# The last queries' scores put ahead of their pair's scores, a head on each half of the array's columns, and the second batch's attention begun 1.5 steps later

## The chip, the cores and the metric

The kernel runs on one core of a Trainium2 chip. The metric is the time of one execution on the device in microseconds (us). Of the kernel before there are three timed runs, with a median of 1007.72 us (1007.47 to 1007.87), and one profiled execution.

## The reference

Two stages follow each other: attention with a sliding window of 128 positions, then a two-layer MLP.

```python
B, H, S, D = 8, 8, 576, 64
scores = (1 / sqrt(D)) * q @ k.T                 # per batch and head
scores += slopes[h] * -abs(i - j)                # a slope per head
scores = where((i - j >= 0) & (i - j < 128), scores, -1e9)
attn = exp(scores - max(scores)); attn /= sum(attn) + 1e-9
x = (attn @ v), heads side by side               # 4608 tokens x 512
h = x @ w_in                                     # 512 -> 2048
g = h * tanh(softplus(h))                        # "mish"
out = g @ w_out                                  # 2048 -> 512
```

## The kernel before, in words

**Work and tiles.** The 576 tokens of a batch are cut into 512 and 64 left over. A *chunk* of the MLP is the 512 tokens of one batch; the 64 that are left of all eight batches make up a ninth chunk. Each chunk runs `first` (its products are called `h`, 8 steps), then `mish`, then `second` (products `po`, for two halves of the tokens: 32 calls of six matmuls, which are the *steps* of the schedule). Both layers take each f32 number as two parts (`parts`, tile `gg`; for the weights `convert`, tiles `si` and `so`), three products each. The weights come as 64-bit words and are turned into these parts by ScalarE (ACT), VectorE (DVE) and GpSimd (POOL) at the start, beside the first batch's attention, the first layer of chunk 0, and the first 11 steps or so of its second layer.

**Attention.** Heads go in four pairs `p`. A pair has two *units* (`unit(b, p, half)`): half 0 takes the first 256 queries, half 1 the next 256, and each unit its own two PSUM banks (tag `s`, two buffers, which `first` uses too). `last_unit(b, p)` takes the 64 queries left over, both heads in one go: the weights `z` (tile `qd`) hold the two heads' queries in opposite corners of a 128x128 square with zeros elsewhere, so that a product with the stacked keys of both heads gives head 0 in rows 0 to 63 and head 1 in rows 64 to 127. From batch 1 on its scores lie in the first 96 columns of the two banks of the pair's half 0, which that unit leaves free. A unit's stages: scores (TensorE, PE), a reduction on DVE that adds the bias and finds the maximum (`exps`: tiles `pz`, `mx`), the exponential on ACT, `fold` and `scale` (in batch 1 on POOL; from batch 2 on by DVE, whose instructions write `un` as well, and ACT), `weights` (four transposes on PE into the scores' own bank, `s<-ident,pz`, and a DVE product with the masks back into `pz`), `values` (PE, `o`), `split_x`.

**Order.** Attention of batch c+1 runs beside `second` of chunk c. `attention` gives each stage a time in units, the main loop maps it to steps by `begin` and `units`, and the work is recorded in order of these times. PE and the DMA queue of SyncE (SP) keep this order; a scheduler places DVE, ACT and POOL instructions, except while the weights are converted. From batch 2 on, both halves' scores of a pair stand together: half 0, half 1, last unit. I call this group of scores a *visit*. In batch 1 half 1's scores come a unit later. Tiles of the last units carry an `l`: `pz_1l`, `pt_1l`.

Every operation is recorded through `InOrder`, so in the profile all have line 30; instructions are told apart by their tiles. A group `64*128` or `128*64` is a matmul that uses half of the array's rows or half of its columns.

Of the kernel before, what the change touches and what calls it, by code (L numbers as in the profile page):

```python
# [8 lines left out]
F32 = mybir.dt.float32  # L9
# [7 lines left out]
P = 128  # L17
# [24 lines left out]
def attention_mish_mlp(  # L42
# [35 lines left out]
    ps = ctx.enter_context(tc.tile_pool(name="ps", bufs=1, space=bass.MemoryType.PSUM))  # L78
# [12 lines left out]
    for t in vb:  # L91
# [8 lines left out]
    pe, dve, act, pool, sp = engines = [  # L100
        InOrder(tc, e, e in (nc.tensor, nc.sync))
        for e in (nc.tensor, nc.vector, nc.scalar, nc.gpsimd, nc.sync)
    ]
# [97 lines left out]
    qkv = {}  # L201
# [42 lines left out]

    HEAD = [slice(i * D, (i + 1) * D) for i in range(2)]

    def unit(b, p, half):


# [4 lines left out]
        st = {}  # L254
        blocks = (0, 1) if half == 0 else (2, 3)
        name = f"{b}_{p}_{half}"

        def scores():
            qk = qkv[(b, p)][0]
            if b == 0 and (2 * p + half) % 3 == 2:  # L260
                s_ = [ps.tile([P, 512], F32, tag=f"po{i}", name=f"s{name}{i}") for i in range(2)]
            else:
                t = ps.tile([P, 2, 512], F32, tag="s", name=f"s{name}", bufs=2)
                s_ = [t[:, i, :] for i in range(2)]
                if half == 0:
                    qkv[("s", b, p)] = t
            st["s"] = s_
            for a, j in enumerate(blocks):
                n = 256 if j else P
                for i in range(2):  # L270
                    pe.matmul(
                        s_[i][:, 256 * (a + 1) - n : 256 * (a + 1)], lhsT=qk[HEAD[i], 0, j * P : (j + 1) * P],
                        rhs=qk[HEAD[i], 1, (j + 1) * P - n : (j + 1) * P], start=True, stop=True,
                    )
# [92 lines left out]
        times = (0, 0.02, 0.25, 0.7, 0.95, 1.3, 1.99, 2.02)  # L367
        if b == 0:
            times = (0, 0.02, 0.2, 0.75, 0.8, 1.62, 2.3, 2.35)
        elif b > 1:  # L370

            times = (
                (-1, -0.8, -0.7, -0.3, -0.25, 0.7 if p == 1 else 0.65, 0.97, 0.99) if half
                else (0, 0.02, 0.12, 0.4, 0.45, 1.4 if p == 1 else 1.3, 1.96, 1.96)
            )
# [4 lines left out]
    def last_unit(b, p):  # L380

        st = {}
        name = f"{b}_{p}l"

        def scores():
            qk, z = qkv[(b, p)]

            if b == 0:
                st["t"] = ps.tile([P, 512], F32, tag="w", name=f"pt{name}")
                st["s"] = st["t"][:, 192:384].rearrange("p (a n) -> p a n", a=2)  # L390
            else:
                st["s"] = qkv[("s", b, p)][:, :, :96]
            for i in range(2):
                pe.matmul(
                    st["s"][:, i, :], lhsT=z, rhs=qk[:, 1, 384 + 96 * i : 480 + 96 * i],
                    start=True, stop=True,
                )

        def exps():
            mx = at.tile([P, 1], F32, tag="mxl", name=f"mx{name}")  # L400
            sm = st["sm"] = at.tile([P, 1], F32, tag="sml", name=f"sm{name}")
            pz = st["pz"] = at.tile([P, 192], F32, tag="pzl", name=f"pz{name}")
            dve.tensor_tensor_reduce(
                out=pz.rearrange("p (a n) -> p a n", a=2), in0=st["s"],
                in1=nl[:, p, :].rearrange("p (a n) -> p a n", a=2), scale=-SCALE, scalar=3.0e38,
                op0=ALU.add, op1=ALU.min, accum_out=mx,
            )
            act.activation(pz, pz, AF.Exp, bias=mx, scale=-1.0, accum_out=sm)

        def fold():  # L410
            sm, pz = st["sm"], st["pz"]
            act.activation(sm, sm, AF.Copy, bias=1e-9)
            dve.reciprocal(sm, sm)
            un = at.tile([P, 1], F32, tag="unl", name=f"un{name}")
            dve.tensor_tensor_reduce(
                out=pz[:, :64], in0=pz[:, :64], in1=pz[:, P:], scale=sm, scalar=3.0e38,
                op0=ALU.add, op1=ALU.min, accum_out=un,
            )
            act.activation(pz[:, 64:P], pz[:, 64:P], AF.Copy, scale=sm)

        def weights():
            if b:
                st["t"] = ps.tile([P, 512], F32, tag="w", name=f"pt{name}")
            t = st["t"]
            pe.transpose(t[:, :P], st["pz"][:, :P], ident)
            pf = st["pf"] = at.tile([P, 2, 2, 64], F32, tag="pfl", name=f"pf{name}", bufs=1)
            shape = [P, 2, 2, 64]
            dve.tensor_tensor(
                out=pf, in0=t[:, :P].rearrange("p (u i n) -> p u i n", u=1, i=2).to_broadcast(shape),
                in1=masks[:, :, :64].rearrange("p u (i n) -> p u i n", i=1).to_broadcast(shape),  # L430
                op=ALU.mult,
            )

        def values():
            va, vl = qkv[("v", b, p)]
            o = st["t"][:, P : P + LEFT]
            for n, val in enumerate((va[:, 3, :], vl)):
                for i in range(2):
                    pe.matmul(
                        o[HEAD[i]], lhsT=val[:, HEAD[i]], rhs=st["pf"][:, n, i, :],  # L440
                        start=(n == 0), stop=(n == 1), skip_group_check=True,
                    )
            xo = at.tile([P, LEFT], F32, tag="xo", name=f"xo{name}", bufs=5)
            dve.tensor_copy(xo, o)
            sp.dma_start(out=xs[p, :, b * LEFT : (b + 1) * LEFT], in_=xo)

        times = (0.01, 0.5, 0.9, 1.4, 1.995)
        if b == 0:
            times = (0.66, 0.7, 1.1, 1.64, 2.32)
        elif b > 1:  # L450
            times = (0.002, 0.21, 0.5, 1.78 if p == 1 else 1.7, 1.98)
        return list(zip(times, (scores, exps, fold, weights, values)))

    def attention(b):
# [48 lines left out]
    def mish(c, j):  # L503
        f = 2 * (j % 2)
        act.activation(gt[(c, j // 2)][:, f : f + 2, :], hs.pop((c, j)), AF.Mish)
# [58 lines left out]
    def in_order(work):  # L564
        dve.fixed = act.fixed = True
        work()
        dve.fixed = act.fixed = False
# [9 lines left out]
    def convert_at(times, tags, lag, mixed):  # L577
        steps = []
        for m, t in enumerate(times):
            kind, j, a = conv.pop(0)  # L580
            step = convert(kind, j, a, tags[m % len(tags)], mixed and m % 2 == 1)
            steps += list(zip((t - lag, t, t + lag), step))
        return steps
# [7 lines left out]
    for c in range(B + 1):  # L591
        if c == 0:
            act.fixed = True
            steps = convert_at([0.35 * m for m in range(4)], ("po0", "po1"), 0.36, True)
            steps += convert_at([0.35 * m for m in range(4, 22)], ("w", "o"), 0.36, True)
            for j in range(NJ):
                steps += [(j, lambda j=j: first(c, j)), (j + 1.04, lambda j=j: mish(c, j))]
            steps += [(NJ - 1.6, lambda: (parts(c, 0, 0), parts(c, 0, 1)))]
            for _, work in sorted(steps, key=lambda s: s[0]):
                work()  # L600
            load_w(*last_w)
            dve.fixed = act.fixed = False
        else:
            for j in range(NJ):
                if j == NJ - 1:
                    parts(c, 0, 0)
                    parts(c, 0, 1)
                first(c, j)
                mish(c, j)

        n = 4 * NJ
        steps = []
        for m in range(2 * NJ):
            for t in range(2):
                steps.append((2 * m + t, lambda m=m, t=t: second(c, *divmod(m, NJ), t)))
            if m >= 2:
                steps.append((2 * m - 4.1, lambda m=m: parts(c, *divmod(m, NJ))))
        if c == 0:
            for t, work in convert_at([0.3 + 1.35 * m for m in range(len(conv))], ("w", "o"), 1.3, True):
                steps.append((t, lambda work=work: in_order(work)))  # L620
        if c + 1 < B:
            begin, units = (1.4, 8.0) if c else (10.0, 9.0)
            steps += [(begin + (n - 2.1 - begin) / units * s, f) for s, f in attention(c + 1)]
        elif c + 1 == B:
            steps.append((4.5, last_x))
        for _, work in sorted(steps, key=lambda s: s[0]):
            work()
# [63 lines left out]
```

## Time and profile before

| | |
|---|---|
| timed runs, median | 1007.72 us |
| the profiled execution's own time | 1008.28 us |
| its span, first to last instruction | 1006.5 us |
| PE busy | 975.6 us, 97% |
| ACT, DVE, POOL busy | 425.0, 375.4, 262.5 us |
| mean granted clock of TensorE | 0.995 of full speed |

The span is what the views cut up; the 1.8 us around it belong to the execution as well. A row of the timeline merges instructions of one kind that follow each other: its second column runs from the start of the first to the modelled end of the last, so it overlaps the next row, and the distance between two rows' starts is the better measure of what the first one cost.

### The profile page before, as it was taken

To read this page: it belongs to the slowest core of one execution; us is meant where nothing else is said; L and a number is where in the kernel's file an instruction comes from. 1 tells how busy PE (TensorE), PEld (TensorE's weight loads), DVE (VectorE), ACT (ScalarE), POOL (GpSimd) and SP (SyncE) were. 2 spreads that over 40 slices of the span, in tenths; PEclk is the share of its full clock that TensorE was granted. 3 is DMA by queue.
4 is the path that set the end of the run, shared out by engine and by line. 5 is a ranking of instruction groups with operands and counts; after the bars stand their busy time and mean duration, and the time that the engine had idled before them with its cause. 6 is when DMAs were issued, how large, how long until landed. Compare 5 with 4: busy or idle time off the path is not lost.

```text
span 1006.5 us, 14264 instructions
## 1 busy us (share of the span) xinstructions
PE 975.6 (97%) x5280; PEld 783.6 (78%) x5280; DVE 375.4 (37%) x1287; ACT 425.0 (42%) x1117; POOL 262.5 (26%) x230
## 2 busy tenths in 40 slices
PE   6799899999999999999999999999999999999998
PEld 4478677887888778887888788887888788888886
DVE  5797563036600762047402670067304650100000
ACT  5698663245432552245324452264324642321221
POOL 4468752112210321023111221032112211141033
PEclk9999899999999999999999999999999999999999
DMA  8961122003100231012200211022100200000001
GB/s 267 396 218 43 36 88 71 1 25 98 41 33 1 64 99 35 1 42 81 72 1 26 75 61 35 1 64 83 49 1 25 73 26 20 21 21 22 1 5 38
DMA packets 52133, 59.32 MB, mean 59 GB/s; under 512 B 13024, under 2 KB 32608, under 8 KB 52064
## 3 DMA queue, kind: packets, MB, share of 16 engines
q1 hardware_dynamic: 50880, 57.69, 17.8%
q8 instruction: 42, 0.69, 0.3%
q10 hardware_dynamic: 1184, 0.72, 0.2%
q14 instruction: 27, 0.22, 0.1%
HBM read 47.91 MB, written 10.49 MB: 58 GB/s over the span
## 4 chain that ended last, share of the span: by engine, by line
PE 85%; DVE 5%; ACT 4%; DMA 3%; SPq 1%; issue 1%; POOL 1%; ACTq 0%; POOLq 0%
PE h L30 38%; PE po L30 33%; PE s L30 8%; PE o L30 4%; DVE pz L30 3%; ACT pz L30 3%; DMA wi<-in_moe_w_in_dram 2%; DMA wo<-in_moe_w_out_dram 1%; SPq L30 1%; DVE pz_1l L30 1%; ACT gg L30 1%; DMA nb<-in_relb_dram 1%; POOL pz L30 0%; DVE ob L30 0%; DVE ti L30 0%
## 5 line engine op out<-in xcount | busy, mean ns | idle before, releaser
L30 PE MATMUL po<-so,gg 128*128 128x512 f32 x1728 | 421.7, 397 | 0.0
L30 PE MATMUL h<-x,si 128*128 128x512 f32 x1728 | 394.5, 389 | 1.1 <-POOL si L30 1.0
L30 PEld LDWEIGHTS h<-x,si 128*128 128x128 f32 x1728 | 323.9, 188 | 70.1 <-POOL si L30 2.3
L30 PEld LDWEIGHTS po<-so,gg 128*128 128x128 f32 x1728 | 318.9, 189 | 64.6 <-issue 0.7
L30 POOL TENSOR_TENSOR gg<-g,gg 128x512 fp32r<-128x512 f32 x144 | 185.0, 1285 | 675.5 <-ACT gg L30 675.3
L30 DVE CUSTOM_DVE_ANT_0 pz<-s,nb 128x256 f32<-128x256 f32 (+1 forms) x256 | 84.8, 386 | 330.4 <-PE s L30 330.3
L30 ACT ACTIVATE g<-h 128x1024 f32<-128x1024 f32 x72 | 74.1, 1029 | 255.5 <-PE h L30 255.5
L30 ACT ACTIVATE pz<-pz,mx 128x256 f32<-128x256 f32 (+1 forms) x256 | 120.0, 470 | 71.2 <-DVE mx L30 71.2
L30 ACT ACTIVATE gg<-g 128x512 fp32r<-128x512 f32 x144 | 89.8, 625 | 89.2 <-PE po L30 86.1
L30 DVE TENSOR_TENSOR pz<-s,masks 128x1024 f32<-128x1024 f32 x64 | 76.3, 1216 | 7.5 <-PE s L30 5.8
L30 DVE CUSTOM_DVE_ANT_0 pz<-pz,sm 128x128 f32<-128x128 f32 x144 | 62.6, 483 | 1.7
L30 DVE COPY ob<-po 128x512 f32<-128x512 f32 x18 | 12.3, 686 | 128.0 <-PE po L30 128.0
L30 PE MATMUL s<-ident,pz 128*128 128x128 f32 x256 | 43.6, 286 | 10.5 <-POOL pz L30 8.3
L30 ACT ACTIVATE x<-o 128x512 fp32r<-128x512 f32 x32 | 19.0, 594 | 81.0 <-PE o L30 81.0
L30 PE MATMUL o<-pz,va 128*64 128x128 f32 (+1 forms) x560 | 50.9, 322 | 1.4 <-DVE pz L30 1.4
L30 PEld LDWEIGHTS o<-pz,va 128*64 128x64 f32 x560 | 33.6, 136 | 22.7 <-issue 7.3
L30 PE MATMUL s<-qk 64*128 64x128 f32 (+1 forms) x448 | 51.2, 365 | 0.0
L30 PEld LDWEIGHTS s<-ident,pz 128*128 128x128 f32 x256 | 32.1, 143 | 23.4 <-POOL pz L30 10.5
L30 ACT ACTIVATION_READ_ACCUMULATOR pz<-pz,mx 128x1 f32 x256 | 47.9, 187 | 0.0
L30 PEld LDWEIGHTS s<-qk 64*128 64x128 f32 x448 | 36.0, 186 | 7.1 <-issue 3.3
L30 ACT ACTIVATE ob<-po 128x512 f32<-128x512 f32 x18 | 10.7, 597 | 61.0 <-PE po L30 61.0
L30 DVE TENSOR_TENSOR x<-o,x 128x512 fp32r<-128x512 f32 x32 | 22.1, 692 | 12.2 <-ACT x L30 12.2
(134 smaller groups left out, 505.4 us busy)
## 6 DMA issues: line engine op xcount, KB each, us to landing
wi<-in_moe_w_in_dram SPq DMA_DIRECT2D x16, 512.0 KB, 10.8
wo<-in_moe_w_out_dram SPq DMA_DIRECT2D x16, 512.0 KB, 10.2
out_dram<-ob SPq DMA_DIRECT2D x32, 256.0 KB, 2.0
qk<-in_q_dram SPq DMA_DIRECT2D x28, 288.0 KB, 3.0
qk<-in_k_dram SPq DMA_DIRECT2D x28, 288.0 KB, 3.3
va<-in_v_dram SPq DMA_DIRECT2D x28, 256.0 KB, 2.9
first<-in_q_dram SPq DMA_DIRECT2D x4, 288.0 KB, 4.0
first<-in_k_dram SPq DMA_DIRECT2D x4, 288.0 KB, 4.2
```

The source lines that it names most:

```text
L30: ins = method(*args, **kwargs)
```

## The change

Three things change. In `last_unit`, from batch 1 on, the scores are computed by four matmuls with 64 of the weights' columns each (one per head and per bank) in place of two with 128. Their time in the schedule goes from just behind the pair's scores to just ahead of them, and so `last_unit` takes the banks and half 0 picks them up. And batch 1's attention begins at step 11.5 of chunk 0's second layer instead of step 10; its end stays, so a unit gets 18.4/9 steps where it had 19.9/9. Batch 0 keeps its order and its two matmuls.

```diff
+    def score_banks(name):
+        return ps.tile([P, 2, 512], F32, tag="s", name=f"s{name}", bufs=2)
...
-                t = ps.tile([P, 2, 512], F32, tag="s", name=f"s{name}", bufs=2)
+                t = qkv.pop(("s", b, p), None) or score_banks(name)
                 s_ = [t[:, i, :] for i in range(2)]
-                if half == 0:
-                    qkv[("s", b, p)] = t
...
+                parts = [slice(0, P)]
             else:
-                st["s"] = qkv[("s", b, p)][:, :, :96]
-            for i in range(2):
-                pe.matmul(
-                    st["s"][:, i, :], lhsT=z, rhs=qk[:, 1, 384 + 96 * i : 480 + 96 * i],
-                    start=True, stop=True,
-                )
+                t = qkv[("s", b, p)] = score_banks(f"{b}_{p}_0")
+                st["s"] = t[:, :, :96]
+                parts = HEAD
+            for a in range(2):
+                for r in parts:
+                    pe.matmul(
+                        st["s"][r, a, :], lhsT=z[:, r], rhs=qk[:, 1, 384 + 96 * a : 480 + 96 * a],
+                        start=True, stop=True, skip_group_check=True,
+                    )
...
-        times = (0.01, 0.5, 0.9, 1.4, 1.995)
+        times = (-0.001, 0.5, 0.9, 1.4, 1.995)
...
-            times = (0.002, 0.21, 0.5, 1.78 if p == 1 else 1.7, 1.98)
+            times = (-0.01, 0.21, 0.5, 1.78 if p == 1 else 1.7, 1.98)
...
-            begin, units = (1.4, 8.0) if c else (10.0, 9.0)
+            begin, units = (1.4, 8.0) if c else (11.5, 9.0)
```

On PE, at the start of batch 1's attention in chunk 0 (`so_951` to `so_953` are the last three pieces of the second layer's weights, `s_0_0` and `s_0_1` the banks of pair 0's two halves, `pt_0l` the last unit's transpose), the kernel before has:

```order
L30 MATMUL s_0_0_1094<-qk_0_390 128x128 x2
L30 MATMUL s_0_0_1094<-qk_0_390 128x256 x2
L30 MATMUL s_0_0_1094<-qk_0_390,qd_83 128x96 x2
L30 MATMUL po_0_1_972<-so_951,gg_0_5_1037 128x512 x6
L30 MATMUL po_0_0_959<-so_952,gg_0_6_1058 128x512 x6
L30 MATMUL s_0_1_1143<-qk_0_390 128x256 x4
L30 MATMUL s_0_0_1094<-ident,pz_0_0_1103 128x128 x4
L30 MATMUL po_0_1_972<-so_952,gg_0_6_1058 128x512 x6
```

The changed kernel has at the same place on PE, from the same point of the second layer on:

```order
L30 MATMUL po_0_1_972<-so_951,gg_0_5_1037 128x512 x6
L30 MATMUL s_0_0_1102<-qk_0_390,qd_83 64x96 x4
L30 MATMUL s_0_0_1102<-qk_0_390 128x128 x2
L30 MATMUL s_0_0_1102<-qk_0_390 128x256 x2
L30 MATMUL po_0_0_959<-so_952,gg_0_6_1058 128x512 x6
L30 MATMUL po_0_1_972<-so_952,gg_0_6_1058 128x512 x6
L30 MATMUL s_0_1_1151<-qk_0_390 128x256 x4
L30 MATMUL po_0_0_959<-so_953,gg_0_7_1085 128x512 x6
L30 MATMUL s_0_0_1102<-ident,pz_0_0_1113 128x128 x4
```

Two steps of `po` have moved ahead of the first transposes, the second of them with `so_953`; between the scores of `s_0_0` and these transposes three steps stand where two stood.

On PE in a visit of batch 2 (pair 1; `qd_84` marks the last unit's scores), before:

```order
L30 MATMUL pt_0l<-pf_0l,vb_87 64x64 x2
L30 MATMUL s_1_0_2028<-qk_1_1543 128x128 x2
L30 MATMUL s_1_0_2028<-qk_1_1543 128x256 x2
L30 MATMUL s_1_1_2033<-qk_1_1543 128x256 x4
L30 MATMUL s_1_0_2028<-qk_1_1543,qd_84 128x96 x2
L30 MATMUL po_0_1_1866<-so_950,gg_0_4_1941 128x512 x6
```

And the same visit on PE now:

```order
L30 MATMUL pt_0l<-pf_0l,vb_87 64x64 x2
L30 MATMUL s_1_0_2035<-qk_1_1551,qd_84 64x96 x4
L30 MATMUL s_1_0_2035<-qk_1_1551 128x128 x2
L30 MATMUL s_1_0_2035<-qk_1_1551 128x256 x2
L30 MATMUL s_1_1_2047<-qk_1_1551 128x256 x4
```

The last unit's scores went from the end of the visit to its start, as four matmuls; from batch 2 on nothing else moved on PE.

On DVE, the reductions behind that visit, before (a row in brackets waits for a semaphore):

```order
L30 ISA pz_1_0_2042,mx_1_0_2040<-s_1_0_2028,nb 128x256
L30 ISA mx_1_0_2040 128x1
L30 ISA pz_1_1_2059,mx_1_1_2057<-s_1_1_2033,nb 128x256 [waits DVE_49]
L30 ISA mx_1_1_2057 128x1
L30 ISA pz_1_1_2059,mx_1_1_2057<-s_1_1_2033,nb 128x256
L30 ISA mx_1_1_2057 128x1
L30 ISA pz_1l,mx_1l<-s_1_0_2028,nl 128x192
L30 ISA mx_1l 128x1
```

And the reductions on DVE behind that visit now:

```order
L30 ISA pz_1_0_2054,mx_1_0_2052<-s_1_0_2035,nb 128x128 [waits DVE_49,PE_49]
L30 ISA mx_1_0_2052 128x1
...
L30 ISA pz_1l,mx_1l<-s_1_0_2035,nl 128x192
L30 ISA mx_1l 128x1
L30 ISA pz_1_1_2071,mx_1_1_2069<-s_1_1_2047,nb 128x256 [waits DVE_49,PE_49]
L30 ISA mx_1_1_2069 128x1
```

The last unit's reduction stands before half 1's, and half 1's has a wait of its own for PE, which it did not have: before, the wait of half 0's first reduction covered the whole visit.

## Rows read from the trace of the kernel before

**Rows 1.** The page: busy time of each engine; the chain that ended last, by engine.

```profile
PE 975.6 (97%) x5280; PEld 783.6 (78%) x5280; DVE 375.4 (37%) x1287; ACT 425.0 (42%) x1117; POOL 262.5 (26%) x230
...
PE 85%; DVE 5%; ACT 4%; DMA 3%; SPq 1%; issue 1%; POOL 1%; ACTq 0%; POOLq 0%
```

**Rows 2.** Timeline of PE, rows with idle time: start, us, engine, operation, [idle <-releaser].

```profile
116.87 1.11 PE L30 MATMUL s<-ident,pz 128*128 128x128 f32 x4 [4.30 <-POOL pz L30]
...
150.07 0.65 PE L30 MATMUL s<-ident,pz 128*128 128x128 f32 x4 [0.56 <-POOL pz L30]
```

**Rows 3.** Waits of PE from 200 us to the end: us in total, times, longest.

```profile
PE s L30 <- DVE un L30: 2.2, 6, 0.4
PE o L30 <- DVE pz L30: 1.4, 6, 0.2
```

**Rows 4.** Stretches: us, busy time of PE, PEld, DVE, ACT, POOL, PEclk, DMA, GB/s.

```profile
112.50:115.50 3.00, 0.07 (x2) 0.00 (x0) 0.87 (x5) 2.77 (x10) 2.89 (x3) 1.00 0.58 183
115.50:122.30 6.80, 5.43 (x16) 4.36 (x17) 3.48 (x11) 2.86 (x10) 5.86 (x6) 0.50 0.04 11
```

**Rows 5.** Timeline of PE behind that idle time, and the same work in batch 2.

```profile
117.63 2.91 PE L30 MATMUL po<-so,gg 128*128 128x512 f32 x6
...
120.41 2.52 PE L30 MATMUL po<-so,gg 128*128 128x512 f32 x6
...
253.96 0.60 PE L30 MATMUL s<-ident,pz 128*128 128x128 f32 x4
254.31 1.64 PE L30 MATMUL po<-so,gg 128*128 128x512 f32 x6
...
256.25 1.63 PE L30 MATMUL po<-so,gg 128*128 128x512 f32 x6
```

**Rows 6.** Timeline of ACT, then of POOL, at the start of batch 1's attention.

```profile
109.37 1.28 ACT L30 ACT_TABLE_LOAD   x1
110.67 0.40 ACT L30 ACTIVATE pz<-pz,mx 128x128 f32<-128x128 f32 x1
...
112.96 0.64 ACT L30 ACTIVATE so<-wo 128x512 fp32r<-128x512 f32 x1
...
112.61 0.73 POOL L30 TENSOR_TENSOR pz<-pz 128x256 f32<-128x256 f32 x1 [2.15 <-ACT pz L30]
...
114.52 1.29 POOL L30 TENSOR_TENSOR so<-wo,so 128x512 fp32r<-128x512 f32 x1
115.77 1.04 POOL L30 TENSOR_TENSOR pz<-pz,sm 128x512 f32<-128x512 f32 x1
```

**Rows 7.** Timeline of DVE and POOL in pair 1 of batch 3.

```profile
348.74 1.43 DVE L30 CUSTOM_DVE_ANT_0 pz<-pz,sm 128x128 f32<-128x128 f32 x1
...
348.72 1.29 POOL L30 TENSOR_TENSOR gg<-g,gg 128x512 fp32r<-128x512 f32 x1 [0.48 <-ACT gg L30]
```

**Rows 8.** Timeline of PE: a visit of batch 3 (pair 2), and rows of batch 1.

```profile
354.67 0.29 PE L30 MATMUL pt_1l<-pf_1l,vb 128*64 128x64 f32 x4
354.89 1.79 PE L30 MATMUL s<-qk 64*128 64x128 f32 x16
356.61 0.69 PE L30 MATMUL s<-qk,qd 128*128 128x96 f32 x4
357.07 7.10 PE L30 MATMUL po<-so,gg 128*128 128x512 f32 x30
...
123.56 0.28 PE L30 MATMUL pt_0l<-pf_0l,va 128*64 128x64 f32 x4
123.67 0.29 PE L30 MATMUL pt_0l<-pf_0l,vb 128*64 128x64 f32 x4
123.89 0.93 PE L30 MATMUL s<-qk 64*128 64x128 f32 x8
...
125.21 1.63 PE L30 MATMUL po<-so,gg 128*128 128x512 f32 x6
...
130.75 1.67 PE L30 MATMUL po<-so,gg 128*128 128x512 f32 x6
```

**Rows 9.** Timeline of DVE: the first reduction behind the visit of rows 8.

```profile
357.33 0.29 DVE L30 CUSTOM_DVE_ANT_0 pz<-s,nb 128x128 f32<-128x128 f32 x1 [1.24 <-PE s L30]
```

## The prediction

> **What bounds the kernel now.** The page comes first: PE is busy for 975.6 of 1006.5 us and holds 85% of the chain that ended last [rows 1]. So time goes only where PE's own work shrinks or where PE stops. The reader should look for PE's stops next, in the timeline of PE with its idle times. Behind the first batch's attention, which this change leaves alone, there are few. Two are in batch 1, 4.30 us and 0.56 us, both ended by POOL's work on `pz` [rows 2]. From 200 us on there are two kinds, once in each of the six later batches: the transposes wait for DVE's `un` (2.2 us in all) and `o` waits for DVE's masks (1.4 us) [rows 3]. The third view is the stretches around the 4.30 us stop: PE is busy for 0.07 of 3.00 us, and then works 6.8 us at a granted clock of 0.50, which is 1.2 GHz in place of 2.4 [rows 4].
>
> What the low clock cost is read from the same work at either level. Four transposes took 1.11 us against 0.60, and six `po` matmuls 2.91 and 2.52 us against 1.64 and 1.63 [rows 2, 5]: 0.51 + 1.27 + 0.89 = 2.7 us. With the two stops, batch 1's attention holds 4.30 + 0.56 + 2.7 = 7.6 us that are not PE's full-speed work.
>
> **Part 1: batch 1 begins 1.5 steps later.** A step is six matmuls, 1.47 us from start to start (125.21 to the next row of its kind; 1.63 with the tail, [rows 8]). In the new order two more steps stand ahead of the first transposes, 2.9 us of work. Does what the transposes wait for come later too? I follow it along ACT and POOL. ACT now issues one `gg` copy ahead of the table load; a copy of this size lasts 0.64 and the next follows after some 0.55 [rows 6], so the load that began at 109.37 begins at about 109.9 and the first exponential at 111.2 instead of 110.67. DVE's reductions, which begin behind two more conversion instructions and the scores, are ready by then at about 110.7, by their own order. The `fold` began 1.94 us behind the first exponential [rows 6]; one `so` copy (0.55) now stands among the exponentials: 111.2 + 1.94 + 0.55 = 113.7. Then POOL has `fold` (0.73), one piece of `so` (1.29) and `scale` (1.04), some 3.0 us: the transposes can start at 116.7. Before it was 116.87. So the chain ends at nearly the same time, and PE brings 2.9 us more work into the gap.
>
> Not all of this is gained. PE stood still from 112.57 (116.87 - 4.30); one step more, 1.47, stands ahead of `so_953`'s first matmul now, so PE reaches it at about 114.0. Its fourth matmul needs POOL's second piece of `so`, which ends at 113.7 + 0.7 + 1.3 = 115.7: a wait of about 0.9 where there was none. Then the transposes wait 0.3. Behind them `pt_0l` needs a DVE instruction with two inputs in SBUF (`un`), and such an instruction that starts while POOL works on a `gg` is held up: 1.43 us at 348.74, as POOL's instruction of 1.29 us began at 348.72 [rows 7]. POOL has two instructions back to back there, so I put 0.8 for it. Stops that remain: 0.9 + 0.3 + 0.8 = 2.0 us, in pieces under 1 us. The bounds are 0.3 (only the transposes' wait) and 4.9 (the old stops at their full length, in other places). I take 2.0 since it is built from the durations.
>
> The clock: it fell behind 3.0 us in which PE was nearly idle [rows 4], and it did not fall around the stop of 0.56 us at 150.07 [rows 2]. Pieces under 1 us with `po` between them are nearer to the second, so I take the 2.7 us as saved. The shorter units that follow (2.04 steps for 2.21) leave one step between each pair of attention stages; half 1's scores stand 7 us ahead of their transposes where before the worst case was about 6, the one with the stop of 0.56. I take that stop as gone. Part 1 gives 7.6 - 2.0 = 5.6 us.
>
> **Part 2: the visits' own PE time.** There are 28 visits (7 batches, 4 pairs); 21 follow a last unit's `pt`, 7 follow `po`. Before: from `pt` (354.67) to the `po` behind the visit (357.07) 2.40 us [rows 8]. After, `pt` and the scores use the same halves of the columns, so there is no change of shape between them. The price of four half-column pairs: four records of 64 columns, two pairs, take 0.11 us (123.56 to 123.67, [rows 8]), so a pair of 96 columns takes 0.055 x 96/64 = 0.083, and four pairs 0.33. The visit after is 0.11 (`pt`) + 0.33 + 0.11 (change to half the rows, as now: 354.89 - 354.67 - 0.11) + 1.72 (the scores with their own change, 354.89 to 356.61) = 2.27. The `po` behind a change of shape lasts a little longer, 1.67 against 1.63 [rows 8]. So a visit gains 2.40 - 2.27 - 0.04 = 0.09 us. In the 7 visits that follow `po` the new scores add a change of shape: 0.33 + 0.11 + 1.72 + 0.04 and about 0.05 for the first pair, 2.25 against 2.18 (354.89 to 357.07), a loss of 0.07. Sum: 21 x 0.09 - 7 x 0.07 = 1.4 us gained. Bounds: 3 us gained if the first pair costs nothing and the pairs run at 64 columns' pace; 16 lost if the halves do not run side by side (rival 3).
>
> **Part 3: the softmax of each visit starts earlier.** This is the part that the diff does not show. DVE's first reduction in a visit waited for the last unit's scores as well: these began at 356.61 and lasted 0.69, to 357.30, and DVE began at 357.33 [rows 8, 9]. Half 0's scores were finished long before. In the new order half 0's reductions wait for half 0's scores alone, and half 1's have their own wait. Half 0's scores begin 0.33 later than now, at 355.2, and eight such records last 0.93 (123.89, [rows 8]): DVE begins at 356.2, 1.1 us earlier, and the exponentials with it. In the visits whose transposes waited, 0.37 us each, and whose `o` waited 0.24 us each 2.2 and 1.4 us over six batches, [rows 3], 1.1 us is more than both. ACT's `gg` copies come later among the exponentials there, but PE needs them over 1 us after POOL has them, by the same durations. So I take 3.6 us as gained. Bounds: nothing, if DVE's `un` instructions meet POOL's `gg` as in [rows 7] at their new times, and a loss of 2 us if pair 0, which has no stop now, gets one of 0.3 in each of six batches.
>
> **The sum.** 5.6 + 1.4 + 3.6 = 10.6 us off the profiled execution's 1008.28 (span 1006.5 and 1.8 around it): 997.7. That execution is 0.56 us above the median of the timed runs, so against 1007.72 it is 997.1. I say 997.
>
> **Rivals.**
> 1. The later begin moves the stop and does not shrink it: PE waits as long for POOL, at `so_953` and behind it, and the clock falls again. For it: the chain through ACT and POOL ends at the same 116.7, and the conversions' last piece is on it. Against it: two steps of work now fill that gap. Then part 1 gives 0.6 at most: 1002.
> 2. The six stops of 0.61 us stay, because the earlier softmax meets POOL's `gg` elsewhere. For it: [rows 7]. Against it: 1.1 us of lead. Then 1000.7.
> 3. The halves of the columns do not run side by side (the slower side). The place is the new scores in each visit, 8 records one behind another at the pace of the old 128-column records (0.46 for 4, 356.61 to 357.07): 0.92 instead of 0.33, 28 x 0.59 = 16.5 us lost, and 1013.5. Below about 0.35 us lost per visit the sum is still a gain. Against it: the records of `pt` have the same shape, and four of them pass in 0.11 us where each lasts 0.28 [rows 8]. On this the Trainium skill has a rule that speaks against the change: by TensorE: Matmul & The Clock Gate, The mechanism, a weight load overlaps running matmuls only when its group of rows differs, and two halves of the columns share all their rows. By that rule the time would be rival 3's; the trace disagrees, since `pt`'s loads fit into 0.055 us a pair.
> 4. No change in effect, gains and new stops cancel: DVE's and POOL's collisions in pairs 0 and 2 eat part 3 and part 1 gives 1 to 2: 1004 to 1006.
>
> **How the numbers follow.** Forecast 60%, its own range 994.5 to 999.5 (part 1's remaining stops between 0.3 and 4, part 2 by 1). Rival 1 13%, rival 2 14%, rival 4 7%, rival 3 6%. The range 993 to 1003 holds the forecast and rivals 1 and 2, and leaves out 3 and 4 and some tails. About 0.2% (2 us) is what a measurement of this kernel can tell from no change. Faster: forecast, rivals 1 and 2 and part of 4, 0.91; same 0.03; slower, rival 3, 0.06.
>
> **What would show it right or wrong.** Right: no stretch at clock 0.50 between 100 and 130 us; PE's stops in batch 1 sum to about 2 us, the first of them inside `po` and ended by POOL's `so`; the list of PE's waits from 200 us on holds no `un`; the records `s<-qk,qd` come in pairs a few ns apart, and from the last `pt` to `po` a visit takes 2.27; DVE's first reduction comes 1.1 us earlier. It would be wrong if the new scores take over 0.6 us a visit, if a new stop stands in pair 0 or 2 of each batch, or if the clock falls again in batch 1.

## The result and the profile after

The changed kernel takes 992.35 us, the median of four runs (991.71 to 992.74), against 1007.80 for the kernel before in the same session (1007.47 to 1007.99). The ratio is 0.9846, with a 95% interval of 0.9829 to 0.9863. Put on the chip again with the later experiments it took 992.04 (991.51 to 992.85), ratio 0.9839 [0.9824, 0.9854]. The prediction of 997 had the sign and the mechanisms, but a third of the gain was missing from its sum, and the time lies 0.65 us below the range's low end.

The page of the changed kernel, busy time of each engine and the chain by engine, answers to [rows 1]. Its span is 989.9 us, the execution's own time 991.71:

```profile
PE 966.7 (98%) x5392; PEld 777.4 (79%) x5392; DVE 372.0 (38%) x1287; ACT 428.8 (43%) x1117; POOL 263.5 (27%) x230
...
PE 93%; DMA 4%; ACT 1%; SPq 1%; POOL 1%; DVE 0%; issue 0%; POOLq 0%
```

PE is still the bound, now with 93% of the chain in place of 85%; DVE's 5% and ACT's 4% of it have shrunk to 0% and 1%. PE has 112 more records (28 visits, 8 half-column matmuls for 4) and is busy for less time.

PE's waits from 100 us to the end (us in total, times, longest) are one row, and answer to [rows 2, 3]:

```profile
PE po L30 <- POOL so L30: 0.8, 1, 0.8
```

From 200 us on the view is empty: neither `un` nor the masks stop PE any more. The two stretches of [rows 4] (columns as there):

```profile
112.50:115.50 3.00, 2.31 (x13) 1.17 (x11) 0.78 (x5) 3.00 (x12) 2.93 (x3) 1.00 0.19 48
115.50:122.30 6.80, 6.67 (x52) 4.82 (x53) 4.95 (x22) 4.14 (x17) 5.82 (x6) 1.00 0.44 155
```

PE works where it had stood still, and the granted clock stays at 1.00. PE's timeline there (start, us, engine, operation, [idle <-releaser]):

```profile
113.74 1.07 PE L30 MATMUL po<-so,gg 128*128 128x512 f32 x3
115.61 0.98 PE L30 MATMUL po<-so,gg 128*128 128x512 f32 x3 [0.80 <-POOL so L30]
116.61 0.66 PE L30 MATMUL s<-ident,pz 128*128 128x128 f32 x4
117.10 0.27 PE L30 MATMUL pt_0l<-ident,pz_0l 128*128 128x128 f32 x1
```

The stop left over is where the prediction put it, at the fourth matmul of `so_953`, and the transposes start at 116.61 (116.7 was foretold, 116.87 before).

**Where the time came from.** A good ruler for this kernel is the first matmul of each chunk's `h`, since the long block of 192 has no stop before or after. For batch 1 the ruler begins at the first `po` of chunk 0, because all that the change moves lies behind it. That `po` and the `h` of chunks 1, 2 and 7, in the kernel before and then in the changed one (the last row of each ends where the view ends):

```profile
92.12 13.08 PE L30 MATMUL po<-so,gg 128*128 128x512 f32 x57
...
167.40 43.68 PE L30 MATMUL h<-x,si 128*128 128x512 f32 x192
277.44 43.68 PE L30 MATMUL h<-x,si 128*128 128x512 f32 x192
...
827.70 2.66 PE L30 MATMUL h<-x,si 128*128 128x512 f32 x11
```

```profile
91.98 13.31 PE L30 MATMUL po<-so,gg 128*128 128x512 f32 x58
...
161.03 43.68 PE L30 MATMUL h<-x,si 128*128 128x512 f32 x192
269.36 43.68 PE L30 MATMUL h<-x,si 128*128 128x512 f32 x192
...
811.08 19.20 PE L30 MATMUL h<-x,si 128*128 128x512 f32 x84
```

Up to chunk 1 the gain is 6.37 us: 0.14 of it lies ahead of chunk 0's first `po`, and 6.23 behind it (167.40 - 92.12 = 75.28 against 161.03 - 91.98 = 69.05). From there to chunk 7 six periods of 110.05 ((827.70 - 167.40) / 6) become six of 108.34, 1.71 less each, 10.24 in all. Behind it both need 178.8 us. 6.37 + 10.24 = 16.6, which is the difference of the spans, 1006.5 - 989.9. (The medians differ by 15.45: the profiled execution of the kernel before, 1008.28, is slower than all four of its timed runs here, and that of the changed kernel is the fastest of its four.) The prediction had 5.8 for the first (part 1's 5.6 and the visits of batch 1) and 4.8 for the second (part 3's 3.6 and the other visits' 1.2). So of the missing 6.0 us 5.4 lie in the six later batches.

**Which stretch of a later batch.** Pair 1 of batch 3, the kernel before and then the changed one, PE's timeline:

```profile
349.58 0.27 PE L30 MATMUL s<-ident,pz 128*128 128x128 f32 x1
350.23 0.87 PE L30 MATMUL s<-ident,pz 128*128 128x128 f32 x3 [0.37 <-DVE un L30]
350.94 0.27 PE L30 MATMUL pt_1l<-ident,pz_1l 128*128 128x128 f32 x1
...
352.52 0.87 PE L30 MATMUL o<-pz,va 128*64 128x256 f32 x8
353.64 1.09 PE L30 MATMUL o<-pz,va 128*64 128x128 f32 x12 [0.24 <-DVE pz L30]
354.56 0.29 PE L30 MATMUL pt_1l<-pf_1l,va 128*64 128x64 f32 x4
```

```profile
341.44 0.60 PE L30 MATMUL s<-ident,pz 128*128 128x128 f32 x4
341.87 0.27 PE L30 MATMUL pt_1l<-ident,pz_1l 128*128 128x128 f32 x1
...
343.46 1.74 PE L30 MATMUL o<-pz,va 128*64 128x256 f32 x20
345.03 0.28 PE L30 MATMUL pt_1l<-pf_1l,va 128*64 128x64 f32 x4
345.14 0.29 PE L30 MATMUL pt_1l<-pf_1l,vb 128*64 128x64 f32 x4
345.26 0.50 PE L30 MATMUL s<-qk,qd 128*64 128x96 f32 x8
345.69 1.79 PE L30 MATMUL s<-qk 64*128 64x128 f32 x16
347.41 2.79 PE L30 MATMUL po<-so,gg 128*128 128x512 f32 x11
```

From start to start the four transposes took 350.94 - 349.58 = 1.36 us and now take 0.43; `o` took 354.56 - 352.52 = 2.04 and now 1.57. That is 0.93 + 0.47 = 1.40 us a batch, where the listed idle times are 0.37 + 0.24 = 0.61. The visit from the last `pt` to `po` went from 2.40 to 347.41 - 345.14 = 2.27. On the mean of the six batches the two stops give 0.92 and 0.46, and three visits 0.135 each. The first visit of a batch, which follows `po`, loses 0.06 (from its first score to the first transposes 9.16 us against 9.10), and the next transposes lose 0.01. Together that is 1.71, the change of the period.

### The profile page after: what moved, and what is told of

Its sections match the earlier page's. It is cut to its first block, busy times and chain, and to the rows that moved or that the text cites. A ratio compares the mean times of both kernels' runs of the same rounds, so it can differ in the third digit from the quotient of the medians.

```text
span 989.9 us, 14477 instructions
## 1 busy us (share of the span) xinstructions
PE 966.7 (98%) x5392; PEld 777.4 (79%) x5392; DVE 372.0 (38%) x1287; ACT 428.8 (43%) x1117; POOL 263.5 (27%) x230
## 4 chain that ended last, share of the span: by engine, by line
PE 93%; DMA 4%; ACT 1%; SPq 1%; POOL 1%; DVE 0%; issue 0%; POOLq 0%
PE po L30 40%; PE h L30 39%; PE s L30 8%; PE o L30 5%; DMA wi<-in_moe_w_in_dram 2%; DMA wo<-in_moe_w_out_dram 1%; SPq L30 1%; DMA nb<-in_relb_dram 1%; DMA first<-in_k_dram 0%; POOL si L30 0%; POOL so L30 0%; PE pt_1l L30 0%; PE pt_3l L30 0%; PE pt_2l L30 0%; PE pt_0l L30 0%
## 5 line engine op out<-in xcount | busy, mean ns | idle before, releaser
L30 DVE CUSTOM_DVE_ANT_0 pz<-pz,sm 128x128 f32<-128x128 f32 x144 | 77.9, 588 | 1.3
L30 PEld LDWEIGHTS o<-pz,va 128*64 128x64 f32 x560 | 33.8, 136 | 19.9 <-issue 6.5
L30 PE MATMUL s<-ident,pz 128*128 128x128 f32 x256 | 39.9, 279 | 3.4 <-POOL pz L30 3.4
```

The source lines that it names most:

```text
L30: ins = method(*args, **kwargs)
```

## The experiments

The kernel before was run again beside each of three sets of experiments (medians 1007.94, 1008.08 and 1008.20). My theory after the result had two parts: the later begin removes the stop and the low clock of batch 1, and the earlier softmax removes pair 1's stops, which cost 1.40 us a batch and not 0.61. The rivals: the column halves make the gain; or the order on PE itself, apart from the softmax; or one of the two parts alone.

**Where batch 1 is measured from.** The profiled executions do not reach chunk 0's second layer at the same time: its first `po` starts anywhere from 91.64 to 93.52 us, though every edit acts behind it. In the run with the begin alone, for one, the granted clock was 0.50 from 43.2 to 50.0 us, where the kernel before had 1.00 from 43.8 on. Why the executions differ there is not shown. What follows goes by that `po`: the pair of `so` pieces ahead of POOL's last two begins 15.75 to 15.77 us behind it in every run, and the changed kernel, traced twice, needs 69.05 and 69.02 us from it to chunk 1's `h`. So batch 1 is compared by this distance (us):

```
                            first po   h of chunk 1   distance
before                        92.12       167.40        75.28
begin alone                   93.52       163.14        69.62
lead alone                    93.03       168.39        75.36
halves alone                  91.64       166.95        75.31
changed kernel, begin 10      92.90       168.40        75.50
own bank                      93.50       167.49        73.99
own bank, begin 11.5          91.76       161.21        69.45
changed kernel                91.98       161.03        69.05
```

The timed runs may carry the same scatter, and each median is of few runs, so differences of up to about 1 us between medians say nothing of batch 1.

**The begin alone.** The kernel before with

```
-            begin, units = (1.4, 8.0) if c else (10.0, 9.0)
+            begin, units = (1.4, 8.0) if c else (11.5, 9.0)
```

> The kernel before with nothing changed but the begin of batch 1's attention (step 11.5 in place of 10). Theory A (the three parts add up, and the later begin is worth what batch 1 gained, 167.40 to 161.03 us at the first h of chunk 1): about 5.5 to 6 us less, near 1002; the stretch at clock 0.50 gone; from chunk 1 on 110.04 us a chunk as before, with pair 1's waits for un. Rival (the later begin only helps because the last unit's scores lead): no gain over 2 us, the stop on POOL still over 3 us.

Measured 1003.25 (1002.67 to 1004.06), ratio 0.9949 [0.9933, 0.9966]. PE's waits from 100 us on:

```profile
PE s L30 <- DVE un L30: 2.2, 6, 0.4
PE o L30 <- DVE pz L30: 1.4, 6, 0.2
PE po L30 <- POOL so L30: 0.6, 1, 0.6
PE po L30 <- ACT so L30: 0.3, 1, 0.3
```

```profile
105.00:125.00 20.00, 19.07 (x112) 13.70 (x111) 13.39 (x46) 15.67 (x45) 17.05 (x15) 1.00 0.18 60
```

Both stops of [rows 2] are gone, and in the stretch from 105 to 125 us the granted clock is 1.00. Pair 1's stops stand as in [rows 3]. The distance from chunk 0's first `po` to chunk 1's `h` is 69.62, 5.66 less than before, and the period is 110.05 still. The span fell by less, 4.3 us, because that `po` itself came 1.40 later in this execution.

**The lead alone.** The last queries' scores go ahead of the pair's, in matmuls over all 128 columns as before, and the begin stays at 10:

```
+                parts = [slice(0, P)]
+            for a in range(2):
+                for r in parts:
...
-        times = (0.01, 0.5, 0.9, 1.4, 1.995)
+        times = (-0.001, 0.5, 0.9, 1.4, 1.995)
...
-            times = (0.002, 0.21, 0.5, 1.78 if p == 1 else 1.7, 1.98)
+            times = (-0.01, 0.21, 0.5, 1.78 if p == 1 else 1.7, 1.98)
```

> The last unit's scores lead the visit, but as two matmuls with all 128 columns; batch 1 begins at step 10 as before. Theory A (in pair 1 of each batch the lead takes away two waits that cost 1.40 us by the distance of starts, 0.61 by the listed idle time): 6 x 1.40 gained, and 28 visits with one more change of the array's shape each, about 0.15 us lost a visit: near 1003.5, a chunk of about 109.2, no waits of PE for un. Rival B (the halves of the columns are what gains): no gain, 1008 or more.

Measured 1003.63 (1002.16 to 1004.38), ratio 0.9953 [0.9938, 0.9969]. The waits hold no `un` and no mask; the stop of batch 1 remains:

```profile
PE s L30 <- POOL pz L30: 4.8, 2, 4.3
```

The period is 109.22 ((823.70 - 168.39) / 6), 0.83 less than before. Of the 1.40 the lead gains, 0.57 are given back, most of it by the full-column scores: a visit behind a `pt` takes 2.55 us (353.67 to 356.23 in batch 3), 0.15 more than before, in three of four visits. They now have a change of shape on both sides. In batch 1 nothing changes (75.36 for 75.28).

**The halves alone.** The half-column matmuls stay behind the pair's scores (`parts = HEAD` in the old place, begin 10):

> The last unit's scores as four half-column matmuls, but behind the pair's scores as before; batch 1 begins at step 10. Theory A: the waits of pair 1 stay (DVE's first reduction still waits for the whole visit), and each visit has one change of shape more for a cheaper block, about +0.04 us: 1008 to 1009, a chunk of 110.1 to 110.3. Rival B (the halves of the columns are what gains): 1000 or less.

Measured 1007.61 (1006.55 to 1008.57), ratio 0.9996 [0.9987, 1.0006]: no difference. Period 110.00; the waits are those of the kernel before:

```profile
PE s L30 <- POOL pz L30: 5.0, 2, 4.3
PE s L30 <- DVE un L30: 2.0, 6, 0.3
PE o L30 <- DVE pz L30: 1.4, 6, 0.2
```

So the halves bring nothing by themselves. They make the lead cheap: with them its period is 108.34, without 109.22. A visit behind a `pt` takes 2.27 us with them and 2.55 without, 0.28 less in each of three visits a batch.

**The changed kernel with the old begin** (11.5 back to 10.0):

> The changed kernel with batch 1's attention begun at step 10 as before. Theory A: chunks 1 to 6 as in the changed kernel, 108.34 us each; batch 1 as before with the stop on POOL (about 4 us) and the low clock: 10.2 us less than before and a few tenths more from batch 1's visits, near 997. Rival (the later begin does nothing by itself): 993 or less.

Measured 999.09 (998.77 to 999.38), ratio 0.991 [0.9895, 0.9925], 2 us above what was expected; of these 0.8 lie ahead of chunk 0's first `po` in the profiled execution. The period is the changed kernel's, 108.33, but the stop in batch 1 is longer than the old one:

```profile
118.91 1.11 PE L30 MATMUL s<-ident,pz 128*128 128x128 f32 x4 [5.30 <-POOL pz L30]
```

POOL's timeline there says why. Behind it stand the `fold`'s rows of the run with the lead alone and of the changed kernel:

```profile
113.41 1.27 POOL L30 TENSOR_TENSOR gg<-g,gg 128x512 fp32r<-128x512 f32 x1 [2.17 <-ACT gg L30]
114.64 1.29 POOL L30 TENSOR_TENSOR so<-wo,so 128x512 fp32r<-128x512 f32 x1
115.89 0.72 POOL L30 TENSOR_TENSOR pz<-pz 128x256 f32<-128x256 f32 x1
116.57 1.29 POOL L30 TENSOR_TENSOR so<-wo,so 128x512 fp32r<-128x512 f32 x1
117.82 1.04 POOL L30 TENSOR_TENSOR pz<-pz,sm 128x512 f32<-128x512 f32 x1
```

```profile
113.50 0.73 POOL L30 TENSOR_TENSOR pz<-pz 128x256 f32<-128x256 f32 x1 [2.10 <-ACT pz L30]
```

```profile
113.56 0.74 POOL L30 TENSOR_TENSOR pz<-pz 128x256 f32<-128x256 f32 x1
```

With the halves in front and begin 10 a `gg` and an `so`, 2.5 us, stand ahead of the `fold` on POOL, where the kernel before had the `fold` first, at 112.61 [rows 6]. (In the changed kernel a `gg` and an `so` stand ahead of the `fold` too, but from 110.29 us on, so that the `fold` is not late.) The lead by itself does not bring this: in the run with the lead in full columns, also with begin 10, the `fold` comes first, and PE's stop is 4.25 us. Why the scheduler, which places POOL's work, chose another order here is not shown. The longer stop costs little in the end: batch 1's distance is 75.50, 0.22 more than before.

**An earlier softmax without the lead.** This is the run that tells the theory from the rival that the order on PE matters. The kernel before with one edit, the last queries' scores in their own unit's bank, so that DVE's first reduction of a pair no longer waits for them; PE's order and shapes are the old ones:

```
-            if b == 0:
-                st["t"] = ps.tile([P, 512], F32, tag="w", name=f"pt{name}")
-                st["s"] = st["t"][:, 192:384].rearrange("p (a n) -> p a n", a=2)
-            else:
-                st["s"] = qkv[("s", b, p)][:, :, :96]
+            st["t"] = ps.tile([P, 512], F32, tag="w", name=f"pt{name}")
+            st["s"] = st["t"][:, 192:384].rearrange("p (a n) -> p a n", a=2)
...
         def weights():
-            if b:
-                st["t"] = ps.tile([P, 512], F32, tag="w", name=f"pt{name}")
```

> The kernel before with one edit: the last queries' scores of batches 1 to 6 go into the unit's own bank, as batch 0's do, and not into the bank of the pair's scores; the order of TensorE's instructions and their shapes stay, and so does the begin of 10. VectorE's first reduction of a pair then waits for the pair's two score matmuls alone. Theory A (pair 1's stops go because the softmax chain begins before the last queries' scores are computed; neither the order on TensorE nor the column halves are needed for it): the releases by `un` vanish from TensorE's waits from 200 us on, the chunk period falls from 110.05 to some 108.65 (1.40 less), the time is near 999.5. Rival B (the chain begins earlier only because TensorE issues the scores earlier; the bank decides nothing): period 110.0, the stops stay, 1007 to 1008. Rival C (the chain gains only in part): between, near 1003.5, with stops under half of the 2.2 and 1.4 us.

Measured 999.67 (997.67 to 1001.04), ratio 0.9917 [0.9901, 0.9934]. The view of PE's waits from 200 us on is empty, and chunks 1, 2 and 7 stand at

```profile
167.49 43.68 PE L30 MATMUL h<-x,si 128*128 128x512 f32 x192
276.19 43.68 PE L30 MATMUL h<-x,si 128*128 128x512 f32 x192
...
819.81 10.36 PE L30 MATMUL h<-x,si 128*128 128x512 f32 x45
```

a period of (819.81 - 167.49) / 6 = 108.72: 1.33 less than before, for stops whose listed idle is 0.61. The softmax does begin earlier. In batch 3 the last `pt` ahead of pair 2's visit starts at 352.09, and DVE's first reduction 1.34 us behind it, where the kernel before took 2.66 [rows 8, 9]:

```profile
353.43 0.28 DVE L30 CUSTOM_DVE_ANT_0 pz<-s,nb 128x128 f32<-128x128 f32 x1
```

The order on PE is not needed for it. Batch 1 gains 1.29 (a distance of 73.99 for 75.28) and no more, since the own bank must first be emptied by the conversion of the weights, and the low clock comes again. PE's row with the wait, and the stretch behind it (columns as in [rows 4], granted clock 0.52):

```profile
112.23 1.17 PE L30 MATMUL pt_0l<-qk,qd 128*128 128x96 f32 x4 [2.75 <-DVE wo L30]
```

```profile
112.20:118.40 6.20, 6.17 (x18) 4.67 (x18) 3.22 (x8) 4.42 (x16) 4.43 (x5) 0.52 0.00 0
```

**Own bank and begin 11.5.** Both edits on the kernel before:

> The kernel before with the last queries' scores in the unit's own bank and batch 1's attention from step 11.5; TensorE's shapes and the order inside a visit stay as before. Theory A (the changed kernel's gain is the earlier softmax plus the later begin, and its order on TensorE is only one way to the first): period 108.73 as in the kernel with the own bank alone, so 6 x 0.39 = 2.3 us more than the changed kernel's 108.34 makes, and batch 1 as in the changed kernel: 994 to 996. Rival B (batch 1 at step 11.5 needs the lead on TensorE too, as the begin alone left stops of 0.26 and 0.64 there): 996.5 to 998.

Measured 994.55 (994.27 to 995.34), ratio 0.9864 [0.985, 0.9879]: theory A. Batch 1's distance is 69.45, 0.40 more than in the changed kernel, and the period is 108.74. So a kernel with PE's old order and shapes has all of the gain but 2.5 us (against 992.04 beside it): 0.40 us in each of six periods, and the rest in batch 1.

**Other begins of the changed kernel**, to look for a better one:

> The changed kernel with batch 1's attention beginning at step 11.0. At 10 the transposes of the first unit waited 5.30 us at 118.91, at 11.5 the only stop is 0.80. If every half step earlier brings back as much of that as the scheme of steps says, a stop of 0.5 to 2.5 us stands at the first transposes, at full clock, h of chunk 1 comes at 161.5 to 163.5, and the time is 993 to 995.5. Rival (11.0 still leaves the chain of the softmax time enough, and the 0.8 us at `so` goes because the order there is another): 991 to 992.3.

> The changed kernel with the begin at 11.25: on TensorE the first unit's transposes stand ahead of the matmuls of the last unit's first half, which waited 0.80 us for `so` in the changed kernel. Either the transposes fill that wait (stop under 0.3, h of chunk 1 0.5 to 0.8 earlier than in the changed kernel of the same call, 991 to 992), or they wait themselves for the softmax of their unit (0.5 to 1.5 us, 992.5 to 994).

> The changed kernel with batch 1's attention beginning at step 12.0 in place of 11.5. Theory (the begin is right when the unit's last wait for GpSimd's `so`, 0.8 us in the changed kernel, is gone, and nothing else in the chunk becomes late): that stop falls under 0.3, the first matmul of chunk 1's h comes 0.5 to 1.0 us earlier than 161.03, the time is 991.4 to 992.2. Rival (the work moved out is missed at the end of the batch: its units come later than the steps that take them up, and a stop appears there): h later than 161.5, 993 to 996.

> The changed kernel with batch 1's attention beginning at step 12.5. Theory: as at 12.0, no wait for `so` is left in TensorE's stops between 105 and 120 us, 991.2 to 992. Rival: the units crowd into the last steps of the batch, TensorE stops for the softmax near 155 to 161 us, 993 to 997.

The period stays 108.33 in all four; only batch 1's part moves (times are medians of four runs each, the distance is that from chunk 0's first `po` to chunk 1's `h`):

```
begin    10.0   11.0    11.25   11.5            12.0    12.5
us       999.09 993.89  994.37  992.35, 992.04  993.88  995.75
distance 75.50  70.31   70.37   69.05, 69.02    70.57   72.56
```

At 11.0 and 11.25 the first transposes wait 2.65 and 2.75 us for POOL's `pz`, longer than expected, so both hopes that a half step or less would fill the 0.8 us fell. The granted clock stays at 1.00 behind these two stops, though behind the 2.75 us of the run with the own bank it was 0.52: in these runs the length of the stop alone does not decide it. At 12.0 the transposes wait 1.71 us for `pz`, and `po` still waits 0.54 for `so`. At 12.5 PE stops at three of the following units:

```profile
PE s L30 <- POOL pz L30: 2.9, 3, 1.4
PE po L30 <- POOL so L30: 1.0, 2, 0.8
PE o L30 <- DVE pz L30: 0.8, 1, 0.8
```

The units are pressed into fewer steps there, and several wait for their own softmax. Expected were gains of up to 1 us at 12.0 and 12.5; the times are the rivals'. Their place is so only in part: the stop at 12.0 is at the first unit and not at the end of the batch, and those at 12.5 stand from 125 to 157 us. No version beat the changed kernel.

## Why the prediction was wrong in its size

**The step that failed is part 3's term, "0.37 us each" and "0.24 us each" for the stops of pair 1.** That the diff would remove them by an earlier softmax was right: DVE's first reduction comes 346.67 - 345.14 = 1.53 us behind the last `pt`, before 357.33 - 354.67 = 2.66 [rows 8, 9], 1.13 earlier where 1.1 was foretold:

```profile
346.67 0.29 DVE L30 CUSTOM_DVE_ANT_0 pz<-s,nb 128x128 f32<-128x128 f32 x1
```

Only their price was read from the wrong column. The list counts idle time from the modelled end of the matmul before, 0.27 us behind its start, while undisturbed transposes start 0.11 apart. So the first stop, listed as 0.37, held PE for 350.23 - 349.58 - 0.11 = 0.54. Behind it the row with x3 hides more: its transposes start 0.27 us apart, as DVE's rows that write `un` do (350.09, 350.37, 350.64), each waiting for its own, and took 350.94 - 350.23 = 0.71 us where three take some 0.33. That is 0.38 more, inside a row that shows as busy, and the two make the 0.93. For `o` it is 0.47 against 0.24. By the run with the own bank the six batches gain 6 x 1.33 = 8.0 us where 3.6 stood: 4.4 us, most of what was missing. Part 3's bounds (a loss of 2 to the 3.6) were too narrow for the same reason: the listed idle was taken as a ceiling, though part 1 had priced a step by starts (1.47 us).

**In batch 1 the earlier softmax is worth little.** With the begin at 11.5 the own bank shortens the distance from 69.62 to 69.45, 0.17 us. The single gains, in the order in which the runs stack them, are 5.66 (begin), 0.17 (softmax, batch 1), 7.86 (softmax, later batches, 6 x (110.05 - 108.74)), 0.40 + 2.40 = 2.80 (lead and halves on PE in place of the own bank), and the 0.14 ahead of chunk 0's first `po`: 5.66 + 0.17 + 7.86 + 2.80 + 0.14 = 16.6, all that was measured.

**Part 1** gave 5.6. The begin alone brought 5.66, and with visits and softmax batch 1 gained 6.23. The mechanism held step by step: the `fold` began at 113.56 (113.7), the transposes at 116.61, the clock stayed high. The stops left were 2.0 by the sum. By starts, with three `po` at 0.74 (half of the 1.47 for six), they are 115.61 - 113.74 - 0.74 = 1.13 at `so_953`, 116.61 - 115.61 - 0.74 = 0.26 ahead of the transposes and 117.10 - 116.61 - 0.43 = 0.06 at `pt_0l`: 1.45 in all, since the 0.8 that I put for an `un` held up by POOL did not come. With some 0.3 for the visits 7.6 - 1.45 + 0.3 = 6.45, 0.2 above what was measured.

**Part 2** was right in the visit (2.27 foretold and measured) and a little too careful around it. Each visit behind a `pt` was charged 0.04 for a longer `po`, which did not come: it gains 0.135 and not 0.09. The first visit of a batch was charged 0.07, and it does lose 0.06. That makes 3 x 0.135 - 0.06 = 0.34 a batch where the sum had 0.2, some 0.9 us more over six batches. The changed kernel's period is 0.40 shorter than that with PE's old order and the own bank (108.74 to 108.34); the other 0.06 are pair 0's transposes, which take 0.50 us with the own bank and 0.44 or 0.45 without.

**The rivals.** Rival 1 (the stop moves and stays) is refuted by the one short stop that is left, 0.80 us, and the clock at 1.00 behind it. Rival 2 (the six stops stay) is refuted by the empty view of waits from 200 us on, and so is rival 4 (gains and new stops cancel), as no stop stands in pairs 0 and 2. Rival 3 is refuted by the halves: eight records in 345.69 - 345.26 = 0.43 us, change of shape included, where the sum had 0.33 + 0.11. This also stands against the rule of the Trainium skill that was weighed there (TensorE: Matmul & The Clock Gate, The mechanism): loads for the two column halves, which share their rows, do pass beside running matmuls here, since the pairs start some 0.083 us apart while each record lasts 0.25. The same section of the Trainium skill also lets a load pass that goes to a background weight buffer, a case that was not weighed; no run tells whether it is the one here. The collision of [rows 7] did not go away, as a DVE row of the changed kernel's batch 3 shows; it lies early enough now that nobody waits for it:

```profile
338.75 1.41 DVE L30 CUSTOM_DVE_ANT_0 pz<-pz,sm 128x128 f32<-128x128 f32 x1
```

## What to carry to other kernels

Price a stop of a pipelined engine by the distance of starts against an undisturbed copy of the same work, not by the listed idle time (1.38 against 0.61 us a batch here): that is counted from a modelled end, and a group of instructions that each wait for a short while reads as busy. Before an order is rewritten, ask whether a consumer waits for more than it reads: here one buffer shared with a later write held the whole softmax back, and a buffer of its own brought about half of the gain without moving an instruction on PE. Where two streams are interleaved on several engines, the start of one has an optimum (here with a loss of 1.3 us at half a step earlier and 1.5 at half a step later). Whether it moves with each change of order was not tried. And before positions of two executions are compared, find the last point that no edit can reach and measure from there: here it moved by up to 1.9 us between executions.

## What the runs showed that was not expected

The half-column matmuls behind the pair's scores are worth nothing (0.9996 [0.9987, 1.0006]), though in front of them they save 0.28 us in each visit that follows a `pt`. By starts 0.10 of it lies between the last `pt` and the scores (0.12 us in place of 0.22), where no change of shape is needed, and the rest in the scores themselves (0.43 in place of 0.61). And with the lead, the halves and the old begin together PE's stop in batch 1 grew from 4.30 to 5.30 us, because POOL worked on a `gg` and an `so` ahead of the `fold`. The lead in full columns alone kept the `fold` first and the stop at 4.25.
